# Attention and snake feed-forward on one Trainium2 core: a rebuilt opening (queries loaded first, keys in three parts, bias bands read from SBUF)

## The chip, the cores and the metric

The kernel runs on one core of one Trainium2 chip. The metric is the device time of one execution in microseconds (us); lower is better. A core has five engines with their own instruction streams: TensorE (PE in the profile, its weight loads PEld), VectorE (DVE), ScalarE (ACT), GpSimd (POOL) and SyncE (SP). Loads and stores are DMA transfers; here SP, ACT and POOL issue them, each on its own queue, and the 16 DMA engines of the core carry them out. SBUF is the on-chip memory with 128 partitions, PSUM the eight banks into which TensorE writes.

## The reference

Attention with a relative position bias over 8 batches, 8 heads, 576 positions and 64 dimensions per head, and a feed-forward layer with the snake activation behind it. In short:

```python
scores = q @ k.T / sqrt(64)                        # [8, 8, 576, 576]
scores = scores + bias_table[bucket(|i - j|)]      # 32 buckets, one value per head
attn = softmax(scores)
x = (attn @ v) as [8 * 576, 8 * 64]                # 4608 tokens, 512 wide
h = x @ w_in                                       # 512 -> 2048
g = h + sin(alpha * h)**2 / (alpha + 1e-9)
out = g @ w_out                                    # 2048 -> 512
```

All inputs and the output are float32 in HBM; the kernel computes in float16 with float32 sums. From a distance of 128 on, all positions fall into the last bucket. So exp(score + bias) is computed as exp(score) times a factor exp(bias - bias of the last bucket) that differs from 1 only in a band around the diagonal: the bias costs one multiply of each tile's band.

## The kernel before, in words

**Blocks.** The outer loop `t` runs over the 8 batches. For each: transposed keys and queries (`kTs`, `qTs`, with two heads, a "pair", on the 128 partitions), scores, exponentials, band multiply, product with `v`, normalization, and a transposed result in `xT`; then w_in, sine, square and g for 512 tokens, and w_out. Scores are computed with keys on the partitions. Unit "A" of a pair is one chunk of 128 keys against 512 queries for both heads, its exponential has 1024 columns (L749). Unit "C" takes the last 64 keys of both heads at once, through a block-diagonal copy `kts` of these keys (the key tail). Batch 0 has four pairs with four A units and one C unit each: twenty exponentials.

**Opening of batch 0.** The keys and then the queries of heads 0 and 1 are loaded on SP (`load_nat`, L475) as float32 with six rows on each of 96 partitions, cast to float16 (`cast0` at L510 and the copies at L558, L559), turned by six TensorE transposes (`plan_tr`, L594) and copied out of PSUM (L583). Pairs 1 to 3 come through POOL's queue already cast (`load_pair`, L475) and are turned at L600. Meanwhile ACT turns the bias table into `e_sb`: eight partitions, one per head, with 512 factors as a function of the distance (`plan_table`; the exponential at L639, the copy at L649).

**Bands.** A multiply needs the factor of key p and query x at every place, which depends on x - p alone. So partition p of the band tile `m2r` has to hold the row of `e_sb` shifted by p. Such a skewed view is a matter of addresses: L650 writes `e_sb` to HBM five times over (`e_dram`), and L516 and L523 read it back with a step of 1 per partition: three loads for `m2r`, two for `mhr` (the bands of the key tail). These five are issued on SP, and behind them the float32 values of heads 4 to 7 (`load_v32`, L462), which POOL casts (L465).

**Order.** The order of instructions on each engine is computed when the program is built. `Plan` holds tasks with the engines that may run them, an estimated duration, dependencies, a priority (lower goes first) and an earliest time `nb`. A list scheduler places them on the estimated clock of each engine; each engine then runs its list strictly in that order, and waits where an input is not there. Constants named `T_...` are the earliest times (of loads that the plan does not model), `WARM...` govern padding matmuls on zeros (`zz`) that fill gaps of TensorE in the opening, and `pad` puts such matmuls behind a task. A task's DMA issues go to the queue of their engine in the order in which the tasks are placed. The attention of batch 0 is laid out in `plan_att0`: a fixed list of units (`runs`), then one product with `v` per pair (`plan_av`), whose last steps are the normalization (L1056, L1057), four transposes (L1088) and a copy into `xT` (L581, L583). In the later batches that transposition is done by a DMA from SP (L1079).

**Behind the opening.** The first w_in matmul of batch 0 is placed at `T_W0` or later; POOL issues the weights (`load_w_in16`, L481) at `T_WI`, after a small copy that waits for band 2 of `m2r` (L675), and the keys and queries of batch 1 (`loads2`) at `T_RST`.

Of the kernel before, what the change touches and what calls it, by code (L numbers as in the profile page):

```python
# [224 lines left out]
WARM_END = 22.0  # L225
# [9 lines left out]
T_CL = 24.5  # L235
# [6 lines left out]
T_V0 = (5.8, 6.4, 8.9, 9.6)  # L242
T_P3 = 7.0
T_VA = (10.5, 11.0)
T_VB = 19.5
V_AT = {1: (4, 5, 6, 7)}
V_PRI = -1000
T_AL = (10.0, 560)
# [3 lines left out]
T_TP = ((150, 150), (650, 650), (1500, 1500))  # L252
# [3 lines left out]
T_LD = 33.0  # L256
# [4 lines left out]
PRE = -100  # L261
# [8 lines left out]
T_WS = (43.0, 48.3, 48.3, 48.3)  # L270
# [7 lines left out]
NORM0 = 900  # L278
SQ = {"ACT": 0.51, "DVE": 0.355}
T_V = ((15.5, 19.0), (50.0, 50.0))  # L280
T_TR1 = ((32.0, 33.5), (35.0, 36.5))
T_W = (25.5, 30.5)
T_WO = (40.5, 43.0, 45.7, 48.3)
WARM0 = 8
# [3 lines left out]
WARM_FROM = 7.3  # L288
# [19 lines left out]
def kernel(  # L308
# [11 lines left out]
    nc = tc.nc  # L320
# [14 lines left out]
    NE = 5  # L335
# [8 lines left out]
    e_dram = nc.dram_tensor("e_dram", [NE, 4 * H, EW], F16, kind="Internal")  # L344
# [50 lines left out]
    )  # L395
    nat2x = tp.tile([128, NF * DM], F16, name="nat2", tag="g", bufs=2)
# [30 lines left out]
    def bank(b, n=1):  # L427
        k = b.banks[0]
        return pb[:, k, :] if n == 1 else pb[:, k : k + n, :]
# [43 lines left out]
    def load_nat(dst, h0, h1, src, eng):  # L473

        eng.dma_start(out=dst, in_=src[h0:h1].rearrange("h (p i) d -> p h (i d)", i=SI))  # L475
# [33 lines left out]
    def cast0(kq, eng):  # L509
        eng.tensor_copy(  # L510
            out=natb[:, kq], in_=nat0[:, kq].rearrange("s two (i d) -> s i two d", i=SI)
        )

    def load_m2r(eng, h0, h1, r):

        eng.dma_start(  # L516
            out=m2r[:, h0:h1],
            in_=bass.AP(tensor=e_dram, offset=EW * (4 * H * r + h0), ap=[[1, 128], [EW, h1 - h0], [1, XW]]),
        )

    def load_mhr(eng):
        for z in range(2):
            eng.dma_start(  # L523
                out=mhr[64 * z : 64 * z + 64],
                in_=bass.AP(tensor=e_dram, offset=EW * (4 * H * (1 + z) + z) + 192,
                            ap=[[1, 64], [2 * EW, NP], [1, 192]]),
            )
# [28 lines left out]
    cast0(0, nc.vector)  # L556
    x0 = nat0[:, 1].rearrange("s two (i d) -> s i two d", i=SI)
    nc.vector.tensor_copy(out=natb[:, 1, :, 0], in_=x0[:, :, 0])  # L558
    P_.tensor_copy(out=natb[:, 1, :, 1], in_=x0[:, :, 1])  # L559
# [70 lines left out]

    def plan_table():
# [12 lines left out]

        def mm(e):
            full(bank(b)[0:H, 0:EW], tabE, phi_sb, True, True)

        def cp(e):
            nc.scalar.activation(out=e_sb, in_=bank(b)[0:H, 0:EW], func=AF.Copy)  # L649
            nc.scalar.dma_start(  # L650
                out=e_dram.ap()[:, 0:H].rearrange("r h x -> h r x"),
                in_=e_sb.unsqueeze(1).to_broadcast([H, NE, EW]),
            )
# [8 lines left out]
        plan.add({"ACT": 1.1}, cp, [x], -1100, use=[b])  # L662
# [144 lines left out]
    def plan_att0(g, gates, gate):  # L807
# [3 lines left out]
        runs = ((a, "A", 0), (a, "A", 1), (a, "A", 2), (a, "C", 0), (a, "A", 3),  # L811
                (b, "A", 0), (b, "A", 1), (b, "C", 0), (b, "A", 2), (b, "A", 3))
        exps, head = [], []
        for i, unit in enumerate(runs):
            base = PB + 3200 * g + 300 * i
# [189 lines left out]
    def plan_av(t, parts, u, ub, done, base, dma):  # L1005
# [457 lines left out]
    tr = {(0, 0, kq): plan_tr(0, 0, kq, -1000, T_FIRST[kq]) for kq in range(2)}  # L1463
# [97 lines left out]
```

## Time and profile before

| | us |
|---|---|
| median of three runs | 364.12 |
| lowest and highest | 364.03, 364.92 |
| profiled execution, first to last instruction (span) | 361.6 |
| median less span | 2.5 |
| TensorE busy, all of the span | 356.0 |
| ACT busy, all of the span | 316.3 |
| DVE busy, all of the span | 306.1 |
| POOL busy, all of the span | 93.2 |

The profiled execution's own time is not listed apart from the span; what lies around the span is taken as the 2.5 us of the table. In the profile a row of the time line reads: start, duration, engine, line, operation, output <- inputs, shapes, count, and in brackets the idle time of the engine just before and what ended it. SPq, POOLq and ACTq are the DMA issues on these engines. A group such as "x14" joins neighbouring instructions of one kind; its duration runs from the first start to the last end. A row of the DMA issues ends with the median time from issue to landing. TensorE's busy time counts matmuls in flight, so that a full engine may still wait briefly. The granted clock of TensorE was 1.00 throughout.

### The profile page before, as it was taken

The page shows a single profiled execution, that of the slowest core. Times are in us where ns is not written, and L with a number is a line of the kernel's source. Part 1 is how long each engine was busy: PE and PEld are TensorE (multiplying, and loading weights), DVE is VectorE, ACT ScalarE, POOL GpSimd, SP SyncE. Part 2 cuts the span into 40 slices and gives each one's busy share as a digit, 9 for nine tenths or more (in the row PEclk, how much of TensorE's full clock was granted, in tenths as well). Part 3 has the DMA queues.
Part 4 walks back from the last instruction along what each step waited for, and adds up shares of the span by engine and source line. Part 5 has one row for each costly group of instructions (what it writes and reads, how often), then busy time and mean ns, then how long its engine had stood idle before and what let it go on. Part 6 is the DMA issues. An engine that isn't in the chain of part 4 may idle for free.

```text
span 361.6 us, 9613 instructions
## 1 busy us (share of the span) xinstructions
PE 356.0 (98%) x3811; PEld 218.4 (60%) x3811; DVE 306.1 (85%) x749; ACT 316.3 (87%) x436; POOL 93.2 (26%) x135
## 2 busy tenths in 40 slices
PE   8999999999999999999999999999999999999996
PEld 4564445644575447884684458545787467456685
DVE  4887888989977998699978997899869986999982
ACT  2998999999998999899989999899989998996811
POOL 8577450064000820055001900091006000000000
PEclk9999999999999999999999999999999999999999
DMA  9999999789724994299918992699339322001023
GB/s 167 206 200 188 207 160 134 142 83 124 120 48 104 138 150 101 55 158 143 137 34 159 110 169 55 127 136 143 87 81 158 66 57 54 15 3 59 31 76 101
DMA packets 150157, 40.53 MB, mean 112 GB/s; under 512 B 137224, under 2 KB 145504, under 8 KB 150112
## 3 DMA queue, kind: packets, MB, share of 16 engines
q0 software_dynamic: 96064, 17.67, 60.7%
q1 hardware_dynamic: 53872, 22.16, 26.1%
q8 instruction: 30, 0.49, 0.6%
q10 hardware_dynamic: 176, 0.09, 0.1%
q14 instruction: 15, 0.12, 0.1%
HBM read 37.73 MB, written 16.56 MB: 150 GB/s over the span
## 4 chain that ended last, share of the span: by engine, by line
PE 94%; DMA 2%; ACT 1%; DVE 1%; SPq 0%; issue 0%; DVEq 0%
PE pb L500 93%; DMA mhr<-e_dram 1%; ACT u L749 1%; DMA e_dram<-e_sb 1%; PE pb L600 1%; PE pb L1088 1%; DVE u L780 1%; DVE s L1057 0%; SPq L523 0%; ACT e_sb L649 0%; PE pb L594 0%; ACT xT L581 0%; SPq L516 0%; DVE outs L1314 0%; DVE zz L551 0%
## 5 line engine op out<-in xcount | busy, mean ns | idle before, releaser
L749 ACT ACTIVATE u<-pb 128x1024 f16<-128x1024 f32 (+1 forms) x146 | 136.8, 1020 | 6.2 <-PE pb L500 4.9
L500 PE MATMUL pb<-xT,w_in 128*128 128x512 f16 (+4 forms) x704 | 128.6, 340 | 0.3 <-ACT xT L581 0.3
L1146 DVE SCALAR_TENSOR_TENSOR g<-sq,inv_a,pb 128x512 f16<-128x512 f16 x144 | 101.4, 744 | 3.8 <-ACT sq L1139 1.8
L1132 ACT ACTIVATE s<-pb,alphaT 128x512 f16<-128x512 f32 x144 | 92.9, 693 | 12.4 <-PE pb L500 11.6
L500 PEld LDWEIGHTS <-w_in 128*128 128x128 f16 x704 | 64.5, 98 | 56.0 <-issue 0.8
L500 PE MATMUL pb<-w_out,g 128*128 128x512 f16 (+1 forms) x416 | 83.5, 339 | 0.0
L500 PEld LDWEIGHTS <-g 128*128 128x128 f16 x552 | 50.8, 98 | 34.8 <-issue 5.2
L780 DVE TENSOR_TENSOR u<-u,m2r 128x512 f16<-128x512 f16 (+1 forms) x128 | 61.5, 488 | 9.9 <-ACT u L749 9.2
L500 PEld LDWEIGHTS <-u 128*128 128x128 f16 x1280 | 55.9, 97 | 9.6 <-issue 4.9
L1139 ACT ACTIVATE sq<-s 128x512 f16<-128x512 f16 x76 | 47.5, 640 | 2.0 <-DVE g L1146 1.1
L445 POOL COPY kt<-kT 64x256 f16<-64x256 f16 x12 | 5.2, 430 | 168.0 <-DMA kT<-staged_k 167.7
L500 PE MATMUL pb<-v,u 128*128 128x65 f16 x1024 | 43.8, 193 | 0.0
L500 PE MATMUL pb<-qT,kT 64*128 64x64 f16 (+1 forms) x512 | 42.1, 285 | 0.8 <-DVE qT L583 0.3
L1141 DVE TENSOR_TENSOR sq<-s 128x512 f16<-128x512 f16 x68 | 28.4, 427 | 11.3 <-ACT s L1132 10.4
L500 PEld LDWEIGHTS <-kT 64*128 64x128 f16 x512 | 17.2, 94 | 20.5 <-issue 13.1
L500 PE MATMUL pb<-vh,u 128*128 128x130 f16 x128 | 28.3, 221 | 0.2 <-DVE s L1057 0.2
L1000 DVE TENSOR_TENSOR xn<-pb,rd 128x384 f16<-128x384 f32 (+2 forms) x53 | 26.0, 490 | 1.8
L450 POOL DMA_DIRECT2D v<-in_v_dram x28 | 24.7, 895 | 3.1 <-DMA nat<-in_k_dram 1.8
L1459 ACT ACT_TABLE_LOAD x15 | 19.2, 1283 | 0.3
L749 ACT ACTIVATE nat<-pb 128x1024 f16<-128x1024 f32 (+1 forms) x24 | 18.8, 820 | 0.0
L999 DVE RECIPROCAL rd<-pb 128x6 f32<-128x6 f32 (+2 forms) x53 | 9.9, 187 | 8.2 <-PE pb L500 7.0
L500 PE MATMUL pb<-wsum,g 128*128 128x256 f16 (+1 forms) x136 | 16.7, 267 | 0.0
(100 smaller groups left out, 311.7 us busy)
## 6 DMA issues: line engine op xcount, KB each, us to landing
out_dram<-outs SPq DMA_DIRECT2D x28, 256.0 KB, 3.0
v<-in_v_dram POOLq DMA_DIRECT2D x28, 128.0 KB, 4.8
staged_k<-in_k_dram POOLq DMA_DIRECT2D x6, 576.0 KB, 8.6
staged_q<-in_q_dram POOLq DMA_DIRECT2D x6, 576.0 KB, 12.1
w_in<-in_moe_w_in_dram POOLq DMA_DIRECT2D x4, 512.0 KB, 9.1
w_out<-in_moe_w_out_dram POOLq DMA_DIRECT2D x4, 512.0 KB, 13.5
out_dram<-outs SPq DMA_DIRECT2D x16, 128.0 KB, 1.7
w_out<-in_v_dram SPq DMA_DIRECT2D x6, 128.0 KB, 5.1
```

The source lines that it names most:

```text
L445: nc.gpsimd.tensor_copy(out=kts[t % 2][r, :, r], in_=kTs[t % 2][r, :, 512:S])
L450: nc.gpsimd.dma_start(out=vs[t % 2][:, c, :, 0:D], in_=vp[128 * c : 128 * c + 128],)
L500: nc.tensor.matmul(out=out, lhsT=lhsT, rhs=rhs, start=start, stop=stop, skip_group_check=go_on)
L749: nc.scalar.activation(out=o, in_=x, func=AF.Exp, scale=0.125)
L780: nc.vector.tensor_tensor(out=io, in0=io, in1=m2[:, 2 * p : 2 * p + 2, x0 : x0 + hi - lo], op=ALU.mult)
L999: nc.vector.reciprocal(out=r, in_=x[:, :, :, D])
L1000: nc.vector.tensor_tensor(out=xn[:, 0:n].rearrange("p c (z d) -> p c z d", z=2), in0=x[:, :, :, 0:D], in1=r.unsqueeze(3).to_broadcast([128 ...
L1132: nc.scalar.activation(out=s16.v, in_=h.v, func=AF.Sin, scale=alphaT[:, f : f + 1])
L1139: nc.scalar.activation(out=sq.v, in_=s16.v, func=AF.Square)
L1141: k_of(e).tensor_tensor(out=sq.v, in0=s16.v, in1=s16.v, op=ALU.mult)
L1146: nc.vector.scalar_tensor_tensor(out=gcell[b].v[:, f, :], in0=sq.v, scalar=inv_a[:, f : f + 1], in1=h.v, op0=ALU.mult, op1=ALU.add,)
L1459: nc.scalar.preload_act_table_set(name)
```

## The change

Only the opening is touched, and constants of the order.

- The queries of heads 0 and 1 are loaded first, then the keys in three parts: rows 0 to 143 and 144 to 287 with two rows on each of 72 partitions, and the remaining 288 with four rows. alpha's load moves from ACT's queue to SP's, behind them; the constants' load on ACT goes ahead of the table's.
- `plan_first` replaces `cast0` and `plan_tr` for pair 0. The query cast is split over DVE and ACT, and so is the copy of the turned queries. Key parts 0 and 1 are cast on DVE, part 2 on POOL; part 0 is copied by ACT, the others by DVE. The key tail's copies move from POOL to DVE. The first exponential needs the queries and key part 0, the second part 1 as well, and only from the third on the whole of the keys.
- `e_dram` and its write are gone. Each head's band is read directly out of its row of `e_sb` by a DMA with the skewed address pattern: eight for `m2r`, eight for `mhr`, all on SP, ahead of the values of heads 4 to 7.
- The order of units in a pair is A, A, C, A, A for all pairs of batch 0.
- For pairs 0 and 1 of batch 0 (`DT0 = 2`) the four TensorE transposes and the copy into `xT` are replaced by one DMA transpose on SP.
- Five instead of eight padding matmuls of 512 columns at the start; earliest times and priorities are set anew, most behind the opening by 2.0 us earlier.

```diff
-WARM_END = 22.0
+WARM_END = 20.0
-T_START = 4.0
+T_START = 3.4
-T_W0 = 24.5
+T_W0 = 22.5
-T_WI = 16.8
-T_TAB = 5.2
+T_WI = 13.4
+T_TAB = 4.0
-T_FIRST = (4.75, 5.95)
-T_PAIR = ((7.9, 8.5), (9.3, 10.2), (11.6, 12.3))
+E_ON = {"ACT": 0.52}
+T_Q0 = 3.95
+T_KP = (4.3, 4.6, 5.2)
+K_CAST = ({"DVE": 0.26}, {"DVE": 0.26}, {"POOL": 0.9})
+K_COPY = ("ACT", "DVE", "DVE")
+K_PRI = (-1880, -1870, 10)
+DT0 = 2
+RUN0 = 'aacaa aacaa'
+U0 = 200
+T_PAIR = ((6.6, 7.2), (8.8, 9.4), (11.0, 11.6))
-T_M2 = (14.6, 15.4, 16.6, 17.2)
-T_MH = 15.4
-T_RST = 25.0
+T_M2 = (9.0, 11.0, 12.5, 12.5)
+T_MH = 10.0
+T_RST = 23.0
-T_VB = 19.5
+T_VB = 17.5
-NORM0 = 900
+NORM0 = 1700
-WARM0 = 8
+WARM0 = 5
-WARM_FROM = 7.3
+WARM_FROM = 6.0
...
-    e_dram = nc.dram_tensor("e_dram", [NE, 4 * H, EW], F16, kind="Internal")
...
+    def skew(h, off, rows, w):
+
+        x = e_sb[h : h + 1]
+        return bass.AP(tensor=x.tensor, offset=x.offset + off, ap=[[EW, 1], [1, rows], [1, w]])
+
+    def load_m2r(eng, h):
+        eng.dma_start(out=m2r[:, h], in_=skew(h, 0, 128, XW))
+
+    def load_mhr(eng, h):
+        z = h % 2
+        eng.dma_start(out=mhr[64 * z : 64 * z + 64, h // 2], in_=skew(h, 192, 64, 192))
...
-    load_nat(nat0[:, 0], 0, 2, k[0], nc.sync)
     load_nat(nat0[:, 1], 0, 2, q[0], nc.sync)
+    for (k0, n_), x in zip(KP, kf):
+        nc.sync.dma_start(
+            out=x, in_=k[0, 0:2, k0 : k0 + SR * n_].rearrange("h (p i) d -> p h (i d)", i=n_)
+        )
+    nc.scalar.dma_start(out=phi_x, in_=phi_h.ap())
     nc.scalar.dma_start(out=tabN, in_=bias_table)
-    nc.scalar.dma_start(out=phi_x, in_=phi_h.ap())
-    nc.scalar.dma_start(out=alphaN, in_=moe_alpha.rearrange("(f p) -> f p", p=128))
+    nc.sync.dma_start(out=alphaN, in_=moe_alpha.rearrange("(f p) -> f p", p=128))
     load_v32(0)
     load_v32(1)
...
+    def plan_first():
...
+        x = nat0[:, 1].rearrange("s two (i d) -> s i two d", i=SI)
+        qs = [cast(natb[:, 1, r], x[:, r], {e: d}, T_Q0, -1990)
+              for r, e, d in ((slice(0, 3), "DVE", 0.36), (slice(3, 6), "ACT", 0.38))]
+        m, q0 = turn([natb[:, 1, i] for i in range(SI)], SN, qTs[0][:, 0, :], qs, -1890,
+                     [("DVE", 0, 3), ("ACT", 3, 6)])
+        m.pad = ((192,) * PAD_FIRST,)
+        ks = []
+        for i, ((a, n), ec, ex) in enumerate(zip(KP, K_CAST, K_COPY)):
+            x = kf[i].rearrange("s two (i d) -> s i two d", i=n)
+            y = cast(kb[i], x, ec, T_KP[i], -1980 + i)
+            m, z = turn([kb[i][:, j] for j in range(n)], SR, kTs[0][:, 0, a : a + SR * n], [y], K_PRI[i],
+                        [(ex, 0, n)])
+            m.pad = ((192,) * PAD_FIRST,)
+            ks.append(z[0])
...
+        tl = plan.add({"DVE": 0.3}, tail, kr, T_TL)
+        tr[(0, 0, 0)] = ks, [tl]
+        tr[(0, 0, 1)] = q0, q0
+        tr["first"] = [ks[:1] + q0, ks[:2] + q0]
...
-            nc.scalar.activation(out=e_sb, in_=bank(b)[0:H, 0:EW], func=AF.Copy)
-            nc.scalar.dma_start(
-                out=e_dram.ap()[:, 0:H].rearrange("r h x -> h r x"),
-                in_=e_sb.unsqueeze(1).to_broadcast([H, NE, EW]),
-            )
-            load_m2r(nc.sync, 0, 2, 0)
-            load_mhr(nc.sync)
-            load_m2r(nc.sync, 2, 4, 3)
-            load_m2r(nc.sync, 4, H, 4)
+            copy_on(e, e_sb, bank(b)[0:H, 0:EW])
+            for p in range(NP):
+                load_m2r(nc.sync, 2 * p)
+                load_m2r(nc.sync, 2 * p + 1)
+                load_mhr(nc.sync, 2 * p)
+                load_mhr(nc.sync, 2 * p + 1)
             for h in range(4, H):
                 load_v32(h)
...
+            if g == 0 and i < 2:
+                deps = gates + tr["first"][i]
...
-        if dma:
+        if dma or wide and p0 < DT0:
 
             def turn(e):
+                if wide:
+                    nc.sync.dma_start_transpose(
+                        out=xT[:, p0, x0 : x0 + 512].rearrange("d (c q) -> d c q", c=4),
+                        in_=xn.v.rearrange("p c d -> p (c d)"))
+                    return
```

`turn` of `plan_first` is the six (or two, or four) transposes of one part with its copies; the units' priorities in `plan_att0` now step by `U0`.

More of the change, by code (lines that the diff above doesn't have):

```diff
@@ L629, in plan_tr, with cast, turn, mm @@
         return [x], [plan.add({"POOL": 0.4 if t == 0 else 0.5}, tail, [x], pri + 30)]
+    def plan_first():
+        def cast(o, i, engs, nb, pri):
+            return plan.add(engs, lambda e: copy_on(e, o, i), [], pri, nb=nb)
+        def turn(parts, rows, dst, deps, pri, copies):
+            b, c = Buf("mo"), Cell()
+            n = len(parts)
+            def mm(e):
+                c.v = bank(b).bitcast(F16)
+                for i, x in enumerate(parts):
+                    nc.tensor.transpose(
+                        out=c.v[:, rows * i : rows * i + rows], in_=x, identity=id_sb[0:rows, 0:rows]
+                    )
+            m = plan.add({"PE": 0.02 + n * T_TURN * rows / 96}, mm, deps, pri, new=[b])
+            made = []
+            for e, a, z in copies:
+                def cp(e, a=a, z=z):
+                    copy_on(e, dst.rearrange("d (p i) -> d p i", i=n)[:, :, a:z],
+                            c.v[:, 0 : n * rows].rearrange("d (i p) -> d p i", i=n)[:, :, a:z])
+                w = (z - a) * rows
+                made.append(plan.add({"DVE": 0.07 + w / 830.0} if e == "DVE" else {"ACT": 0.07 + w / 1150.0},
+                                     cp, [m], pri, use=[b]))
+            return m, made
+        x = nat0[:, 1].rearrange("s two (i d) -> s i two d", i=SI)
[12 more added lines that the diff above has]
+            ks.append(z[0])
+        kr = ks[2:]
+        def tail(e):
+            for z in range(2):
+                r = slice(64 * z, 64 * z + 64)
+                k_of(e).tensor_copy(out=kts[0][r, 0, r], in_=kTs[0][r, 0, 512:S])
+        tl = plan.add({"DVE": 0.3}, tail, kr, T_TL)
+        tr[(0, 0, 0)] = ks, [tl]
+        tr[(0, 0, 1)] = q0, q0
+        tr["first"] = [ks[:1] + q0, ks[:2] + q0]
@@ L1462 @@
     PB = 0
[L1463 removed]
+    tr = {}
+    plan_first()
     vdone, lds, spans = [], [], {}
```

69 lines of the change are left out of this document (30 added, 39 removed).

## The prediction

> **What bounds the kernel now.** I read the page first (busy shares and the chain that ended last), then busy time by stretches, then the opening instruction by instruction.
>
> ```profile
> span 361.6 us, 9613 instructions
> PE 356.0 (98%) x3811; PEld 218.4 (60%) x3811; DVE 306.1 (85%) x749; ACT 316.3 (87%) x436; POOL 93.2 (26%) x135
> ...
> PE 94%; DMA 2%; ACT 1%; DVE 1%; SPq 0%; issue 0%; DVEq 0%
> ```
>
> Busy us by stretches; the columns are PE, PEld, DVE, ACT, POOL, then granted clock, DMA share and GB/s:
>
> ```profile
> 8.45:14.43 5.98, 5.95 (x96) 3.27 (x95) 4.85 (x9) 5.81 (x7) 4.18 (x11) 1.00 1.27 172
> 14.43:19.60 5.17, 4.75 (x58) 2.74 (x58) 4.58 (x13) 5.17 (x7) 3.22 (x6) 1.00 1.03 226
> 33.00:50.00 17.00, 17.00 (x194) 8.25 (x191) 14.97 (x32) 16.74 (x28) 10.80 (x16) 1.00 1.51 193
> 46.00:357.00 311.00, 310.90 (x3300) 193.33 (x3300) 269.79 (x671) 277.97 (x380) 61.59 (x66) 1.00 0.85 100
> ```
>
> The chain lies 94% on PE. PE fills the last 311 us (310.90 of it), so nothing the change touches shortens that part; it can only start it sooner or later. Before it ACT is the full engine: 5.81 of 5.98, 5.17 of 5.17, then 16.74 of 17.00. So the opening is a run of exponentials on ACT, and its worth is when the first one starts, whether the run stays closed, and what follows the last.
>
> ```profile
> 0.81 0.40 SPq L475 DMA_DIRECT2D natx<-in_k_dram  x1
> 1.27 0.43 SPq L475 DMA_DIRECT2D natx<-in_q_dram  x1
> ...
> 3.92 0.64 DVE L510 CAST natx<-natx 96x768 f16<-96x768 f32 x1 [1.15 <-DMA natx<-in_k_dram]
> 4.97 0.69 PE L594 MATMUL pb<-id_sb,natx 96*128 96x96 f16 x6
> 5.32 0.35 DVE L558 CAST natx<-natx 96x384 f16<-96x384 f32 x1 [0.76 <-DMA natx<-in_q_dram]
> 5.35 0.69 POOL L559 CAST natx<-natx 96x384 f16<-96x384 f32 x1 [0.74 <-DMA natx<-in_q_dram]
> 6.74 0.43 PE L594 MATMUL pb<-id_sb,natx 96*128 96x96 f16 x6
> 7.21 0.76 DVE L583 COPY qT<-pb 128x576 f16<-128x576 f16 x1 [0.75 <-PE pb L594]
> 8.02 0.39 PE L500 MATMUL pb<-qT,kT 64*128 64x512 f16 x2 [0.27 <-DVE qT L583]
> 8.45 1.02 ACT L749 ACTIVATE u<-pb 128x1024 f16<-128x1024 f32 x1 [1.01 <-PE pb L500]
> 9.64 11.66 ACT L749 ACTIVATE u<-pb 128x1024 f16<-128x1024 f32 x14 [0.17 <-PE pb L500]
> 21.57 4.26 ACT L749 ACTIVATE u<-pb 128x1024 f16<-128x1024 f32 x5 [0.27 <-PE pb L500]
> 25.66 0.69 DVE L1057 TENSOR_TENSOR s<-pb,rd 128x512 f16<-128x512 f32 x1
> 26.27 0.42 DVE L780 TENSOR_TENSOR u<-u,m2r 128x512 f16<-128x512 f16 x1
> 28.97 5.99 PE L500 MATMUL pb<-xT,w_in 128*128 128x512 f16 x27 [0.26 <-ACT xT L581]
> ```
>
> The queries come second and set the first exponential: cast from 5.32, turned at 6.74, copied at 7.21 to 7.97, multiplied at 8.02, exponential at 8.45. Twenty exponentials end at 21.57 + 4.26 = 25.83, 17.38 us later. From there to the closed run of w_in matmuls (28.97) it is 3.14 us of one chain. The bias bands, the table and the transfers are carried by further views. Who waited for whom on SP, and the DMA issues with their time to landing:
>
> ```profile
> SPq L516 <- DMA e_dram<-e_sb: 7.7, 1, 7.7
> ...
> natx<-in_k_dram SPq DMA_DIRECT2D x1, 288.0 KB, 3.1
> natx<-in_q_dram SPq DMA_DIRECT2D x1, 288.0 KB, 4.0
> tabN<-in_bias_table_dram ACTq DMA_DIRECT2D x1, 1.0 KB, 2.5
> phi_sb<-phi_const ACTq DMA_DIRECT2D x1, 36.0 KB, 3.8
> w_out<-in_v_dram SPq DMA_DIRECT2D x6, 128.0 KB, 5.1
> xT<-xn SPq DMA_TRANSPOSE x47, 2.8
> ```
>
> The instructions in order of time, with the write of the bands' source from the chain as the second line:
>
> ```profile
> 6.85 0.59 ACT L649 ACTIVATE e_sb<-pb 8x512 f16<-8x512 f32 x1 [0.62 <-PE pb L500]
> 7.46 2.94 DMA e_dram<-e_sb
> 10.49 0.37 SPq L516 DMA_DIRECT2D m2r<-e_dram  x1
> 10.90 1.33 SPq L523 DMA_DIRECT2D mhr<-e_dram  x2
> 13.44 3.44 SPq L462 DMA_DIRECT2D w_out<-in_v_dram  x4
> 14.43 1.35 DVE L780 TENSOR_TENSOR u<-u,m2r 128x512 f16<-128x512 f16 x3
> 20.77 0.42 DVE L583 COPY xT<-pb 128x512 f16<-128x512 f16 x1
> 21.09 1.68 POOL L465 CAST v<-w_out 128x256 f16<-128x256 f32 x4
> 24.82 1.02 PE L500 MATMUL pb<-xT,w_in 128*128 128x512 f16 x4
> 26.39 0.74 POOL L475 DMA_DIRECT2D nat<-in_k_dram  x1
> ```
>
> **The change part by part.**
>
> *Queries first.* The first load on SP lands at 0.81 + 3.1 = 3.91 (the cast row agrees: 3.92), the second at 1.27 + 4.0 = 5.27. Queries in first place gain 1.36 us. Half of their cast goes to DVE (0.35, the same size as L558) and half to ACT, which has no such row of its own there; 0.4 by the 8x512 copy's 0.59 as upper end. So 4.35 to 4.5 instead of 6.04 (5.35 + 0.69 on POOL). Six transposes take 0.43 to 0.69: 4.95 to 5.2. The copy, 0.76 for 576 columns, is halved over DVE and ACT, near 0.42: with 0.1 us of hand-over at each step the queries stand near 5.6.
>
> *Keys in three parts.* Rows 0 to 143 and 144 to 287 are 72 KB each and follow the queries at once; 288 KB took 1.36 us between the two landings, so a quarter takes 0.35: about 4.3 and 4.7, the rest 5.3 to 5.7. First part: cast on DVE near 0.25 behind its query half, two transposes, 144 columns copied on ACT behind its query half: 5.9. The first score matmul then stands near 6.0 instead of 8.02, and the first exponential, 0.43 later, near 6.45 instead of 8.45: 2.0 us. The ends: 6.1 if nothing queues, 7.1 if PE stands behind the table. phi now goes out first on ACT's queue and lands at 0.81 + 3.8 = 4.6; the matmul that needs it ranks ahead of all else on PE, so the query transposes may wait until about 5.
>
> *What moves with them.* Two more loads on SP, and alpha's from ACT's queue, push the first two value heads back by 3 x 0.43 = 1.3 us. Their readers are POOL's casts and the first attention product, which waits for bands in any case; no cost. POOL, which issues loads, also gets the third part's cast, 0.9 us (0.69 x 512/384), near 5.6 to 6.6; the loads queued behind it are for pair 3, not wanted before 19. The key tail, now on DVE, must be done for the third exponential (order A, A, C, A, A): 6.6, then four transposes, 288 columns copied, tail 0.3, matmul 0.39, gives about 8.3, where ACT comes free near 8.3. I count 0.1, ends 0 and 0.4.
>
> *Warm-up.* Three 512-column matmuls fewer ahead of the transposes.
>
> ```profile
> 1.26 3.92 PE L500 MATMUL pb<-zz 128*128 128x512 f16 x10 [1.26 <-DVE zz L551]
> ```
>
> These ran near 0.42 us each while two 512-column score matmuls later took 0.39 together, with a granted clock of 1.00 in every stretch. If PE stays at the slow pace to the first score, transposes cost 0.69 instead of 0.43 and two score matmuls 0.85 instead of 0.39: 0.7 us late at most. I take 0, since the loss is only on the first scores and the padding matmuls continue. The Trainium skill (TensorE: Matmul & The Clock Gate, Part 1) asks for about 3.4 us of sustained work before full speed; five matmuls are 2.1 us of it, so by the page the slow case is the likelier, and the sum would be 0.7 us worse.
>
> *Bands from SBUF.* Gone are the write (2.94) and SP's wait for it (7.7). Instead e_sb, copied on ACT in the same 0.59 and now near 6.4, is read directly by sixteen issues. By 0.37 (one with 256 runs) to 0.67 (half of 1.33) each, they hold SP until 12.4 to 17.2, against 13.4 now. The bands need not be early: DVE began them at 14.43 and the last one (26.27) still came right after the last exponential. Behind them on SP stand four value heads (3.44 to issue, then 5.1), read by POOL at 21.09, in the new schedule at 19.1. At the short end the first lands at 12.4 + 5.1 = 17.5, the fourth at about 20.4, as it is cast; at the long end 22.3, which would hold back the products of pairs 2 and 3 by 3 us. A single head has half the runs of the 0.37 row; I take the short end, 0.
>
> *Two pairs turned by DMA.* PE loses eight 128-column transposes, DVE two copies of 0.42. In their place stand 2.8 us of landing. Pair 1 would be there near 23.1, beside a first reader at 24.82 - 2 = 22.8. PE has other work then; 0, ends 0 and 1. SP has nothing else to do at that time except the value heads just named.
>
> *End of the opening.* The last multiply (26.27) sat behind pair 2's normalization (0.69 from 25.66, released by ACT at about 25.9). Normalizations now rank later; 0 to 0.4 gained, I count 0.1. Weights and the next batch are issued earlier (w_in by 3.4 us, the next queries and keys by 2), and their POOL order is otherwise kept: the 26.39 load moves with POOL's free time, 24.4. If it did not move, the transposes that read it would give the gain back.
>
> **Sum.** -2.0 (first exponential) + 0.1 (third) - 0.1 (end) = -2.0, then 0.1 for new small waits: -1.9. Everything behind the opening keeps its length, so the span is 359.7. The profiled execution's time beside its span is not shown apart; the runs' median stands 2.5 above the span, and I keep that: 362.2.
>
> **The rivals.**
>
> *The gain is given back.* The run of exponentials starts early but is opened by a load behind it: value heads late on SP (up to 3 us), the third key part, a cold PE (0.7), or the next batch's keys. For it: DMA share is above 1 in both opening stretches shown. Against it: in the stretch 14.43 to 19.60 ACT never waits although the bands come at 14.43. On 362.2 these put 0.7 to 3 us: about 363.0 to 365.2.
>
> *Bands drip out of a few lines.* Every band is now read from one row of e_sb by all DMA engines at once. The one read of e_sb in the trace is the write of 40 KB in 2.94, 0.44 above the 1 KB load's 2.5: some 90 KB/us from eight rows. All bands are 8 x (96 + 24) = 960 KB; at that rate they take 10.6 us and land between 11.7 and 19.6 (from 6.5 + 2.5), still ahead of pair 3's exponentials. DVE needs about 2.2 us for a pair, so they must be there by 21.8, which is 75 KB/us: below that this rival decides. At half the measured rate, 45 KB/us, the last band lands at 30.3, 8.5 late: 362.2 + 8.5 = 370.7, slower than before. Against it: no row shows a read slowed this way. The Trainium skill (SBUF — State Buffer, Door 1: The DMA port swizzle) has four neighbouring partitions share one port of about 27 GB/s, here heads 0 to 3 on one and 4 to 7 on another; by that, in one queue, 36 us and an end near 386. The 40 KB row is short of settling it, since two such ports would also have passed it in 0.75.
>
> *More than forecast.* The bands' early arrival empties DVE and the tail of 3.14 us shrinks by 0.4 or more: below 361.3.
>
> **How the numbers follow.** Gain carried through 0.64 (361.3 to 363.0), given back 0.16, bands drip 0.17, more 0.03. Three runs differ by 0.9 us, so 0.3% (1.1 us, 363.0 to 365.2) is what counts as a change: faster 0.67, same 0.16, slower 0.17. The range 361.2 to 365.2 leaves out the slow bands and the far gain.
>
> **What would show it.** First exponential at 6.1 to 7.1, the twentieth ending near 23.9, closed w_in matmuls from about 27.0, PE full from there on. Wrong if DVE's first band multiply stands after 12 or the bands' landing grows from head to head (drip); if the value casts on POOL start after 20 (SP queue); if the exponentials show new gaps (third key part, cold PE); or if 27.0 is reached and the stretch behind it, closed now (17.00 of 17.00), shows PE waiting for weights or for the next batch's keys.

## The result and the profile after

| | before | after |
|---|---|---|
| median, us (four runs each) | 364.14 | 394.00 |
| lowest and highest | 364.03, 364.92 | 393.59, 394.61 |
| profiled execution, span | 361.6 | 392.8 |

The ratio is 1.0812, with a 95% interval from 1.0778 to 1.0847: the changed kernel is 8% slower. The forecast was 362.2, and its range ended at 365.2.

The busy shares and the chain that ended last, of the kernel after:

```profile
PE 365.3 (93%) x3799; PEld 223.2 (57%) x3799; DVE 305.2 (78%) x751; ACT 318.6 (81%) x439; POOL 92.2 (23%) x133
...
PE 86%; SPq 8%; DMA 4%; ACT 1%; issue 0%; POOL 0%; ACTq 0%; DVE 0%
```

SP's queue, which rounded to 0% of the chain before, now carries 8% of it. Busy time of the part behind the opening (columns as in the prediction):

```profile
80.00:389.00 309.00, 308.90 (x3268) 192.66 (x3266) 268.05 (x664) 275.16 (x377) 56.97 (x65) 1.00 0.81 99
```

PE fills this part as it did before (308.90 of 309.00, against 310.90 of 311.00). The whole loss lies in the opening. Its instructions in order of time:

```profile
4.15 0.52 ACT L588 ACTIVATE natx<-natx 96x384 f16<-96x384 f32 x1 [1.15 <-DMA natx<-in_q_dram]
4.72 0.24 PE L516 MATMUL pb<-tabN,phi_sb 32*32 32x8 f32 x2 [0.82 <-DMA tabN<-in_bias_table_dram]
5.24 0.69 PE L650 MATMUL pb<-id_sb,natx 96*128 96x96 f16 x6
7.13 0.30 PE L650 MATMUL pb<-id_sb,natx 72*128 72x72 f16 x2
7.24 0.52 PE L516 MATMUL pb<-zz 128*128 128x192 f16 x2
7.69 0.61 PE L516 MATMUL pb<-qT,kT 64*128 64x512 f16 x2
8.07 0.60 POOL L590 CAST natx<-natx 72x512 f16<-72x512 f32 x1 [3.72 <-DMA natx<-in_k_dram]
8.34 1.02 ACT L808 ACTIVATE u<-pb 128x1024 f16<-128x1024 f32 x1 [0.51 <-PE pb L516]
9.10 5.59 SPq L535 DMA_DIRECT2D mhr<-e_sb  x2
10.67 1.02 ACT L808 ACTIVATE u<-pb 128x1024 f16<-128x1024 f32 x1 [1.31 <-PE pb L516]
18.06 0.90 DVE L839 TENSOR_TENSOR u<-u,m2r 128x512 f16<-128x512 f16 x2 [5.68 <-DMA m2r<-e_sb]
29.26 0.42 DVE L839 TENSOR_TENSOR u<-u,m2r 128x512 f16<-128x512 f16 x1 [4.07 <-DMA m2r<-e_sb]
33.74 4.68 SPq L535 DMA_DIRECT2D mhr<-e_sb  x2
38.46 10.23 SPq L478 DMA_DIRECT2D w_out<-in_v_dram  x4
39.10 0.90 DVE L839 TENSOR_TENSOR u<-u,m2r 128x512 f16<-128x512 f16 x2 [6.11 <-DMA m2r<-e_sb]
48.41 0.43 DVE L839 TENSOR_TENSOR u<-u,m2r 128x512 f16<-128x512 f16 x1 [6.76 <-DMA m2r<-e_sb]
60.36 1.84 ACT L1200 ACTIVATE s<-pb,alphaT 128x512 f16<-128x512 f32 x3 [0.48 <-PE pb L516]
```

Line numbers have moved: L531 and L535 issue the bands of `m2r` and `mhr`, L839 is the band multiply, L808 the exponential, L478 the value heads' load, L481 their cast, L588 and L590 copies and casts on ACT and on other engines, L650 the turns of the first pair, L516 any other matmul, L1200 the sine. Read the four L839 rows that wait for `m2r`: they stand some 10 us apart (18.06, 29.26, 39.10, 48.41), one for each pair of heads. SP is held all that time: the issues of the sixteen bands run until 33.74 + 4.68 = 38.42, the four value heads stand behind them, and the first sine, at 29.38 before, starts at 60.36, 31 us later. The list of waits up to 62 us says the same (engine, reader <- what it waited for: total us, times, longest):

```profile
DVE u L839 <- DMA m2r<-e_sb: 22.6, 4, 6.8
...
POOL v L481 <- DMA w_out<-in_v_dram: 10.5, 1, 10.5
PE pb L607 <- DVE alphaT L750: 7.0, 1, 7.0
...
DVE qT L590 <- ACT qT L588: 0.5, 1, 0.5
```

DVE runs its list in order, so what stands behind a band multiply waits with it. The `alphaT` line shows this: a PE matmul is held 7.0 us by a small DVE copy that the bands do not concern. In this way late bands also stop the exponentials on ACT.

And the DMA issues of the kernel after, with the median time from issue to landing at the end:

```profile
m2r<-e_sb SPq DMA_DIRECT2D x8, 96.0 KB, 10.7
mhr<-e_sb SPq DMA_DIRECT2D x8, 24.0 KB, 13.3
```

A pair's bands are 240 KB, and three pairs follow each other from 18.06 to 48.41: 10.1 us each, about 24 KB/us. The prediction's rival of dripping bands decides below 75 KB/us.

One more thing differs from before. The granted clock of TensorE, 1.00 in every stretch of the kernel before, falls here (the third number from the end):

```profile
46.00:60.00 14.00, 7.33 (x90) 5.67 (x90) 4.61 (x12) 2.83 (x5) 7.16 (x18) 0.63 0.60 102
```

It reads 0.50 from 41 to 44 and again from 49 to 57; PE had waited 2.6 us before its work at 40.89 and 5.3 before that at 49.73. So the work behind such a wait also runs slower. Up to 40 the clock reads 1.00, though two scores take 0.61 there (7.69), not the 0.39 of before; this comes back below.

But the bands are one part of a change of many parts. What each is worth, and whether the drip is really a matter of where `e_sb` lies, was tried on the chip.

### The profile page after: what moved, and what is told of

It reads as the page before. It is cut to its first block, busy times and chain, and to the rows that moved or that the text cites. A ratio compares the mean times of both kernels' runs of the same rounds, so it can differ in the third digit from the quotient of the medians.

```text
span 392.8 us, 9616 instructions
## 1 busy us (share of the span) xinstructions
PE 365.3 (93%) x3799; PEld 223.2 (57%) x3799; DVE 305.2 (78%) x751; ACT 318.6 (81%) x439; POOL 92.2 (23%) x133
## 4 chain that ended last, share of the span: by engine, by line
PE 86%; SPq 8%; DMA 4%; ACT 1%; issue 0%; POOL 0%; ACTq 0%; DVE 0%
PE pb L516 84%; SPq L535 5%; DMA w_out<-in_v_dram 4%; SPq L531 2%; DMA tabN<-in_bias_table_dram 1%; PE pb L607 1%; PE pb L1156 0%; ACT u L808 0%; POOL v L481 0%; PE pb L650 0%; ACT e_sb L588 0%; ACTq L548 0%; DVE outs L1382 0%; PE pb L1044 0%
## 5 line engine op out<-in xcount | busy, mean ns | idle before, releaser
L808 ACT ACTIVATE u<-pb 128x1024 f16<-128x1024 f32 (+1 forms) x146 | 137.7, 1015 | 25.2 <-PE pb L516 23.9
L516 PE MATMUL pb<-xT,w_in 128*128 128x512 f16 (+4 forms) x704 | 128.7, 341 | 0.0
L1200 ACT ACTIVATE s<-pb,alphaT 128x512 f16<-128x512 f32 x144 | 92.8, 692 | 12.4 <-PE pb L516 11.6
L516 PEld LDWEIGHTS <-w_in 128*128 128x128 f16 x704 | 64.6, 98 | 55.4
L839 DVE TENSOR_TENSOR u<-u,m2r 128x512 f16<-128x512 f16 (+1 forms) x128 | 61.4, 486 | 31.4 <-DMA m2r<-e_sb 22.6
L516 PE MATMUL pb<-w_out,g 128*128 128x512 f16 (+1 forms) x416 | 83.5, 339 | 0.0
L516 PEld LDWEIGHTS <-u 128*128 128x128 f16 x1280 | 59.5, 101 | 20.9 <-issue 16.5
L516 PEld LDWEIGHTS <-g 128*128 128x128 f16 x552 | 50.8, 98 | 34.8 <-issue 5.2
L516 PE MATMUL pb<-v,u 128*128 128x65 f16 x1024 | 47.2, 199 | 2.9 <-POOL v L481 2.9
L516 PE MATMUL pb<-qT,kT 64*128 64x64 f16 (+1 forms) x512 | 44.8, 297 | 0.0
L516 PE MATMUL pb<-vh,u 128*128 128x130 f16 x128 | 29.4, 230 | 7.9 <-DVE s L1120 7.9
L516 PEld LDWEIGHTS <-kT 64*128 64x128 f16 x512 | 16.9, 95 | 21.2 <-issue 14.2
L1527 ACT ACT_TABLE_LOAD x15 | 19.2, 1283 | 0.3
L808 ACT ACTIVATE nat<-pb 128x1024 f16<-128x1024 f32 (+1 forms) x24 | 18.8, 822 | 0.0
L607 PE MATMUL pb<-id_sb,nat 96*64 96x96 f16 x168 | 7.1, 239 | 11.1 <-DVE alphaT L750 7.0
```

Of the source, the lines that this page charges most:

```text
L516: nc.tensor.matmul(out=out, lhsT=lhsT, rhs=rhs, start=start, stop=stop, skip_group_check=go_on)
L607: nc.tensor.transpose(out=c.v[64 * z : 64 * z + 64, x : x + SN], in_=(nat1 if t == 0 else nat2)[:, kq, h, D * i : D * i + D], identity=id_ ...
L808: nc.scalar.activation(out=o, in_=x, func=AF.Exp, scale=0.125)
L839: nc.vector.tensor_tensor(out=io, in0=io, in1=m2[:, 2 * p : 2 * p + 2, x0 : x0 + hi - lo], op=ALU.mult)
L1200: nc.scalar.activation(out=s16.v, in_=h.v, func=AF.Sin, scale=alphaT[:, f : f + 1])
L1527: nc.scalar.preload_act_table_set(name)
```

## The experiments

Two ladders were run: from the kernel after downwards, one part taken back at a time, and single parts put into the kernel before. The edits are shown abridged; constants of several lines may stand on one.

**Bands by HBM again.** The kernel after with `e_dram`, its write and the five reads of before, and their earliest times.

```diff
-T_WI = 13.4, T_M2 = (9.0, 11.0, 12.5, 12.5), T_MH = 10.0
+T_WI = 16.0, T_M2 = (14.6, 15.4, 16.6, 17.2), T_MH = 15.4
+    e_dram = nc.dram_tensor("e_dram", [NE, 4 * H, EW], F16, kind="Internal")
```

> The changed kernel with one part undone: the bands go through HBM again (five copies written, five loads), with the earliest times that belong to it. Theory (the bands drip because every read of a band goes to one place in SBUF): the drip is gone, DVE's first band multiply stands near 14.5 to 15.5 and the time falls by 28 to 31 us, to 363 to 366. Rival (the other parts cost too: third key part late, cold TensorE, value heads late): the time stays 3 us or more above 366.

Measured: 379.54 (ratio to before 1.0408, 1.0341 to 1.0475). The drip goes, and with it 14.5 us; the other 15 us stay. So the rival held, and by far more than the 3 us it named. DVE's first band multiply stands at 19.94 and not at 14.5 to 15.5. From its time line:

```profile
12.20 0.61 PE L518 MATMUL pb<-qT,kT 64*128 64x512 f16 x2
...
22.06 2.92 POOL L499 DMA_DIRECT2D w_in<-in_moe_w_in_dram  x4
...
27.21 3.93 SPq L1149 DMA_TRANSPOSE xT<-s  x2
...
37.53 1.44 PE L518 MATMUL pb<-xT,w_in 128*128 128x512 f16 x3 [8.41 <-DMA xT<-s]
```

Busy time of one stretch of it (columns as before):

```profile
12.00:16.00 4.00, 4.00 (x26) 1.41 (x24) 1.17 (x5) 3.56 (x4) 1.68 (x4) 1.00 1.07 169
```

Two new suspects: PE waits 8.41 us for a pair turned by DMA, and two score matmuls take 0.61 instead of 0.39 at 12.20, though PE is full in that stretch (4.00 of 4.00) and the granted clock reads 1.00 there.

**Where the bands are read from.** Three kernels that differ in the source partitions alone. `e_sb` is computed alike on all 128 partitions, and a band is read from 128 of them, from eight neighbours, or from eight that lie four apart: bytes, queue and order stay. The skew is left out, so the bands are not the reference's. The last three lines are the three variants:

```diff
-        x = e_sb[h : h + 1]
-        ap=[[EW, 1], [1, rows], [1, w]]          # the change: the one row of head h
+        in_=e_sb[:, 0:XW]                        # row p from partition p
+        ap=[[EW, 8], [1, rows // 8], [1, w]]     # from partitions 0 to 7
+        ap=[[4 * EW, 8], [1, rows // 8], [1, w]] # from partitions 0, 4, ... 28
```

> The changed kernel, with the table copied to all 128 partitions (same instructions, wider operands) and each of the sixteen band loads reading row p from partition p. It leaves the skew out: the bands are not the reference's. Number, size and run length of the transfers are as in the changed kernel. Theory (one place in SBUF is the limit): each band lands in 3 to 5 us, the time is 362 to 367. Rival (sixteen small SBUF to SBUF loads with 768-byte runs on SP's queue are slow by themselves): it stays at 388 or more.

> As the run from 128 rows, but every band is read from the eight neighbouring partitions 0 to 7, sixteen rows from each; skew left out, the bands are not the reference's. Theory (a group of four neighbouring partitions shares one port): two groups, twice the rate of one row, about 50 GB/s in place of 25; all bands take some 20 us instead of 40, the time is 372 to 380. Rival (the single partition is the limit): eight times the rate, the time is as with eight partitions four apart, 362 to 368.

> As the run from eight neighbours, but the eight partitions are 0, 4, 8 to 28: same number of partitions, same runs, same DMA engines, skew left out, the bands are not the reference's. Theory (groups of four): eight groups, so four times the rate of the eight neighbours; the time is 362 to 368. Rival (the single partition is the limit, or the number of DMA engines is): no different from the eight neighbours, within 2 us.

Measured, one run each: 374.96, 381.04 and 374.19; one row for each head, the kernel after, has 394.00. The absolute times lie higher than expected; the runs below take other parts apart that cost too. The differences answer the question: eight rows four partitions apart are as good as 128, eight neighbours cost 6.9 us more, with the same bytes and runs. SP's issues from the time line of the first (128 rows), beside the two that take 5.59 from 9.10 on in the kernel after:

```profile
17.93 1.24 SPq L531 DMA_DIRECT2D mhr<-e_sb  x2
19.22 8.05 SPq L478 DMA_DIRECT2D w_out<-in_v_dram  x4
```

The same of the second (eight neighbours), and DVE's multiplies that wait for its bands:

```profile
9.57 3.77 SPq L535 DMA_DIRECT2D mhr<-e_sb  x2
15.09 0.90 DVE L841 TENSOR_TENSOR u<-u,m2r 128x512 f16<-128x512 f16 x2 [2.76 <-DMA m2r<-e_sb]
20.76 0.42 DVE L841 TENSOR_TENSOR u<-u,m2r 128x512 f16<-128x512 f16 x1 [1.18 <-DMA m2r<-e_sb]
26.29 0.90 DVE L841 TENSOR_TENSOR u<-u,m2r 128x512 f16<-128x512 f16 x2 [1.60 <-DMA m2r<-e_sb]
```

The first three pairs stand 5.6 us apart here, so 240 KB come at about 43 KB/us, not quite twice the 24 from one row. If each partition alone were the limit, eight would give far more than that. So a read out of few neighbouring partitions is slow. The Trainium skill (SBUF — State Buffer, Door 1: The DMA port swizzle) says that four neighbouring partitions share one port of about 27 GB/s; the 24 KB/us (GB/s) from one row, the 43 from two groups of four and the gap between the second and the third kernel agree with it. Even with the port out of the way, the band issues take 0.62 us each (1.24 for two) and start the value heads at 19.2 (128 rows) and 18.7 (eight, four apart) instead of 13.44. That is later than the "long end" of 17.2, where the prediction had taken the short one.

**Bands from SBUF alone**, in the kernel before, the mirror of the first run: `load_m2r` and `load_mhr` as in the diff of the change, the constants as before.

```diff
-            load_m2r(nc.sync, 0, 2, 0); load_mhr(nc.sync); load_m2r(nc.sync, 2, 4, 3); load_m2r(nc.sync, 4, H, 4)
+            for p in range(NP):
+                load_m2r(nc.sync, 2 * p); load_m2r(nc.sync, 2 * p + 1)
+                load_mhr(nc.sync, 2 * p); load_mhr(nc.sync, 2 * p + 1)
```

> The kernel before with one part of the change alone: the bands read from their rows of the table in SBUF by sixteen loads. Theory (a row of SBUF is read at 25 GB/s: 960 KB in 39 us, and four value heads behind it): the time is 386 to 394, and the landings of the bands lie some 9 us apart per pair. Rival (the slow bands of the changed kernel come from what else it loads at that time): 364 to 372.

Measured: 396.38 in one run, 32 us above before and 2 us beyond what the theory named. The part alone costs as much as the whole change. A load of another queue comes late beside it: PE waits for the keys of pair 3, which POOL loads and for which PE did not wait in the kernel before. Its list of waits:

```profile
DVE u L772 <- DMA m2r<-e_sb: 17.6, 3, 8.4
PE pb L498 <- POOL v L463: 13.4, 1, 13.4
...
PE pb L595 <- DMA nat<-in_k_dram: 7.8, 1, 7.8
```

**Bands by HBM, without DMA turns.** The first run above, and all pairs turned by TensorE again.

```diff
-DT0 = 2
+DT0 = 0
```

> The run with bands by HBM (379.5 us), and also the turns of pairs 0 and 1 back on TensorE. In that run TensorE waited 8.4 us for a DMA turn that stood behind the w_in load. Theory (the DMA turns cost what their landing shows): the wait goes and the time falls by 5 to 8 us, to 371 to 375; it is less than 8.4 because the products of pairs 2 and 3 and the w_in landing come next. Rival (w_in itself is what is late, the DMA turn only ended last): within 2 us of 379.5.

Measured: 373.63 (1.0251, 1.021 to 1.0291), 5.9 us less.

**DMA turns alone**, in the kernel before.

```diff
-        if dma:
+        if dma or wide and p0 < DT0:                        # DT0 = 2, as in the change
```

> The kernel before with one part of the change alone: the turns of pairs 0 and 1 by DMA. Theory (a DMA turn issued while w_in is being loaded lands only behind it): the two turns land 6 us or more after their issue, the first w_in matmul waits for them, the time rises by 2 to 6 us, to 366 to 370. Rival (the wait of 8.4 us came from w_in being issued 5 us later there): 363.5 to 364.7, no change.

Measured: 376.65 (1.032, 1.0247 to 1.0392), 12 us above before and more than expected. From its time line:

```profile
18.30 2.93 POOL L482 DMA_DIRECT2D w_in<-in_moe_w_in_dram  x4
...
20.67 5.53 SPq L1079 DMA_TRANSPOSE xT<-s  x2
```

In its view of `xT` in the opening, the time from issue to landing:

```profile
DMA to landing us min/median/max: 10.9/11.0/11.2
```

PE waits 8.5 us for these two. 11 us, where the later batches' turns took 2.8 in the rows of the prediction. Around them POOL issues the 2 MB of w_in (18.30 to 21.23). Is it that load, or the turn itself?

**DMA turns ahead of the weights.** The same kernel with w_in issued behind the turns.

```diff
-T_WI = 16.8, T_W0 = 24.5
+T_WI = 24.0, T_W0 = 29.0
```

> The kernel before with the first two pairs turned by DMA, as in the run of that part alone, but the w_in load issued at 24.0 (placed) instead of 16.8, so behind both turns, and the first w_in matmul placed at 29.0 instead of 24.5. Theory (a DMA turn that is issued behind the 2 MB load of w_in waits for that load's packets on the shared DMA engines): the two turns land within 5 us of their issue instead of 11.0, PE waits less than 1 us for xT from a turn instead of 8.5, and it waits for w_in instead, so that the span is no shorter than the 375.0 of that run by more than 4 us. Rival (a DMA turn in the opening is slow for a reason of its own: the bands, the value heads, its first use): the turns still land 9 us or more after their issue, and PE waits for xT.

Measured: 371.88 in one run (before 364.55 beside it). From its time line:

```profile
20.62 3.73 SPq L1079 DMA_TRANSPOSE xT<-s  x2
...
25.35 2.91 POOL L482 DMA_DIRECT2D w_in<-in_moe_w_in_dram  x4
...
33.27 10.14 PE L501 MATMUL pb<-xT,w_in 128*128 128x512 f16 x34 [1.86 <-DMA w_in<-in_moe_w_in_dram]
```

The landing of the two turns:

```profile
DMA to landing us min/median/max: 2.5/3.3/4.2
```

The turns land in 3.3 us and nobody waits for them: so it was the load of w_in, not the turn itself, that made them slow. PE now waits for the weights (issued 7 us later), and the loss is 7 us instead of 12. The span, 369.9, is 5.1 us shorter than in the run before, a little more than the 4 that the theory allowed. Either order of turns and weights costs.

**Warm-up.** The run by HBM and without DMA turns, and eight starting matmuls instead of five.

```diff
-WARM0 = 5
+WARM0 = 8
```

> As the previous run, and eight padding matmuls of 512 columns at the start in place of five. Theory (with five, TensorE stays at the slow pace: two score matmuls 0.61 us and not 0.39, to 24 us): the score matmuls take 0.39 again from the first on, the run of exponentials shortens by 4 to 5 us, the time falls to 366 to 371. Rival (the pace comes from something else in the new order, such as the half-height score matmuls): no change, within 1 us of the previous run.

Measured: 369.66 (1.0147, 1.0122 to 1.0173), another 4.0 us. The group of the 32 score matmuls in the opening (busy us, mean ns), with five:

```profile
L518 PE MATMUL pb<-qT,kT 64*128 64x512 f16 x32 | 8.5, 549 | 0.0
```

The same group with eight:

```profile
L518 PE MATMUL pb<-qT,kT 64*128 64x512 f16 x32 | 6.3, 414 | 0.8 <-ACT u L816 0.8
```

And from the time line with eight, the exponentials:

```profile
7.81 12.80 ACT L816 ACTIVATE u<-pb 128x1024 f16<-128x1024 f32 x15 [0.59 <-PE pb L518]
```

**Five starting matmuls alone**, in the kernel before.

```diff
-WARM0 = 8
+WARM0 = 5
```

> The kernel before with one edit: five padding matmuls at the start in place of eight. Theory (fewer leave TensorE slow through the opening): the score matmuls show about 0.6 us for two, the time rises by 3 to 5 us, to 367 to 369. Rival (the other paddings make up for it): 364, within 1 us.

Measured: eight executions that fall into two groups, 364.33 to 364.63 (four) and 368.57 to 370.15 (four). The profiled one belongs to the second. From its time line, the matmuls on zeros at the start and the first two scores:

```profile
1.27 2.63 PE L500 MATMUL pb<-zz 128*128 128x512 f16 x7 [1.27 <-DVE zz L551]
...
8.46 0.61 PE L500 MATMUL pb<-qT,kT 64*128 64x512 f16 x2
```

With five, the same kernel takes as long as before or 4 to 5.5 us longer. In the profiled execution two scores take 0.61 up to 24.62 and 0.39 from 25.70 on. No profile of the first group was taken; that TensorE reaches its full pace in time there is inferred from the times. The granted clock reads 1.00 all along, so the slow PE is seen only in the duration of one kind of matmul. (In the run with bands from SBUF alone two scores also take 0.61, at 20.51, where the clock reads 0.50.) The Trainium skill (TensorE: Matmul & The Clock Gate, Part 1) asks for about 3.4 us of sustained work before full speed. The group at the start lasts 2.63 us here and 3.92 in the kernel before, one on each side of that figure; the trace agrees. What lets four of eight executions with five come out fast is open.

**Ranks of the turns.** The last kernel of the ladder with the priorities of pairs 1 to 3 as before.

```diff
-T_TP = ((150, 750), (1150, 1350), (2200, 2400))
+T_TP = ((150, 150), (650, 650), (1500, 1500))
```

> The run with bands by HBM, no DMA turn and eight warm-ups (369.7 us), and the priorities of the turns of pairs 1 to 3 as in the kernel before. In that run ACT stood 3.9 us between the fifteenth and sixteenth exponential: TensorE waited 2.7 us for DVE's copy of pair 3's queries, which the order puts behind eight band multiplies. Theory (the new ranks only suit bands that come early): that wait goes, the time falls by 2 to 4 us, to 366 to 368. Rival (the bands by HBM are late whatever the rank): within 1 us of 369.7.

Measured: 366.14 (1.0045, 1.0014 to 1.0076). With the ranks of the change PE waits for a later pair's queries, and the exponentials, closed until 20.6, show a hole of 3.91 us. The time line of the kernel with eight starting matmuls, ahead of this edit:

```profile
21.64 0.22 PE L518 MATMUL pb<-vh,u 128*128 128x130 f16 x1 [2.69 <-DVE qT L595]
...
24.52 2.43 ACT L816 ACTIVATE u<-pb 128x1024 f16<-128x1024 f32 x3 [3.91 <-PE pb L518]
```

And with the ranks of before:

```profile
21.04 1.94 ACT L816 ACTIVATE u<-pb 128x1024 f16<-128x1024 f32 x2 [1.51 <-PE pb L518]
```

The largest hole is 1.51, and the first sine comes 2.5 us earlier (32.49, not 34.99). The granted clock, 0.50 from 22 to 25 with the ranks of the change, stays at 1.00. The remaining 1.8 us (1.0045) are not taken apart.

**The first pair alone**: queries first, keys in three parts, casts on two engines; everything else as before, but for the earlier start of the plan and of the padding (`T_START`, `WARM_FROM`) and the duration planned for the table's copy (`E_ON`). Then the same with the third key part cast on DVE and the queries copied by DVE in one piece.

```diff
-K_CAST = ({"DVE": 0.26}, {"DVE": 0.26}, {"POOL": 0.9});  [("DVE", 0, 3), ("ACT", 3, 6)]
+K_CAST = ({"DVE": 0.26}, {"DVE": 0.26}, {"DVE": 0.5});   [("DVE", 0, 6)]
```

> One part of the change alone: queries first, keys in three parts, casts and copies on two engines; all else as in the kernel before (bands by HBM, eight warm-ups, order, ranks and times of the later work, turns on TensorE). Theory (this part is worth what the first exponential gains, and the run of exponentials behind it stays closed): the first exponential at 7.6 to 8.0 and not 8.45, the time 363.3 to 363.8, that is 0.3 to 0.8 us less. Rival (the third key part and the key tail open the run by as much): 364.0 to 365.0.

> As the previous run, but the third key part is cast on DVE in place of POOL, and the queries are copied by DVE in one piece (in the changed kernel DVE's half began only when ACT's half was done). Theory (POOL's cast is late because of POOL's issues, and the split copy gains nothing): the key tail comes 0.5 us earlier, the time is the previous run's or up to 0.4 us less. Rival (DVE becomes full): 0.3 us or more above the previous run.

Measured: 372.39 (1.0204, 1.0158 to 1.025) and 367.04 (1.0069, 1.0039 to 1.0099). They start their exponentials at 8.83 and 8.74. The busy time behind the opening, of the first:

```profile
62.00:360.00 298.00, 292.06 (x3074) 180.78 (x3071) 258.59 (x633) 257.39 (x353) 56.91 (x64) 1.00 0.76 95
```

In the second PE is full there (298.00 of 298.00). What stands ahead of the first exponential in the first of the two:

```profile
8.27 0.52 ACTq L717 DMA_DIRECT2D e_dram<-e_sb  x1
8.83 1.02 ACT L816 ACTIVATE u<-pb 128x1024 f16<-128x1024 f32 x1 [0.59 <-PE pb L655]
```

Neither brings the first exponential below the 8.45 of before. Its scores are there in time (at 7.55, for 0.39), but ACT first copies the table (7.65 to 8.24) and issues the write of the bands, until 8.79. The plan expects 0.52 us for both, the value that belongs to the copy without a write; the kernel before plans 1.1. In the second kernel the write's issue ends at 8.70 and the exponential follows at 8.74. So the theory of an earlier first exponential was not put to a fair test, and 8 and 2.7 us are not the price of this part alone.

The first of the two also loses 6 us behind the opening, in holes of PE of up to 0.5 us that the second doesn't have. The edit lies in the first pair alone, but the order of PE's instructions differs between the two over most of the program: the planner's clocks were shifted, and everything later was placed anew. Which of its decisions makes the holes is not settled.

No kernel tried was faster than the one before.

## Why the prediction was wrong

**The ladder.** From 394.0: bands by HBM -14.5, turns by TensorE -5.9, eight starting matmuls -4.0, ranks as before -3.5, remainder 1.8 to 364.3. Single parts in the kernel before: bands +32, turns +12, five starting matmuls 0 or +4 to 5.5, first pair +8 or, with another assignment, +2.7 (with the table's write in its way). These don't add up to 30; that a late band covers part of the other losses is likely, but no run shows it apart.

*The granted clock: no term in the sum.* The prediction had it at 1.00 in every stretch of the kernel before. PE's busy time times the missing share of the clock, added up over the first 80 us, is an estimate of what its fall costs: 4.1 us of the 30 in the kernel after, 7.6 with bands from SBUF alone, 2.8 with DMA turns alone. It is 2.1 with bands by HBM and 0 without the DMA turns, 1.7 with eight starting matmuls and 0 with the ranks as before. By this estimate some 2 us each of the steps of 5.9 and 3.5 are the clock behind a wait, not the wait. Between eight neighbours and eight apart it makes no difference (1.8 and 2.0).

*Bands from SBUF: wrong, and the largest miss.* The failed step is "I take the short end, 0", and under it the estimate of "some 90 KB/us from eight rows". That row was a write of 40 KB in which a fixed time dominates; it was taken as evidence of the rate at which one row can be read. The sum itself holds no term for the time of the reads. The rate was 24 KB/us, the mechanism that of the rival, with 0.17. The rival's own price for a half rate, 370.7, was also too low; the end near 386 that it gave by the port's figure lies closer to the 394.0 measured. SP's hold was predicted too short in the same step: not 0.37 to 0.67 an issue, but 2.8 (half of 5.59) at 9.10, while the transfers ahead of it were slow.

*Two pairs turned by DMA: wrong.* "2.8 us of landing" came from later batches, where nothing like 2 MB of weights stands ahead. In the opening it was 11.0, and 3.3 with the weights moved behind. The step had looked at SP's queue alone, not at what POOL's has in flight at that time.

*Warm-up: wrong.* "I take 0" had as its upper end 0.7, counting only the first scores. The slow pace lasts through most of the opening; the term is 0 or 4 to 5.5 us. That "the padding matmuls continue" doesn't end it: at 12.20, with PE full, the scores still take 0.61.

*Queries first: mostly wrong.* The queries landed nearly as predicted (their cast begins at 4.15, forecast 3.91). The first exponential came at 8.34 instead of 6.45, the gain 0.1 instead of 2.0. The step that failed is the sum "then stands near 6.0 instead of 8.02" with its end "7.1 if PE stands behind the table". PE does stand behind it: the table's product is released by its load at 4.72, and the turns follow at 5.24, forecast 4.95, at 0.69. Then DVE's half of the queries waits 0.5 us for ACT's and is done at 6.97. The first score still has to wait: ahead of it PE takes the turn of the second key part (7.13) and that turn's two padding matmuls (7.24, 0.52), which the sum had left out. It stands at 7.69 and takes 0.61. With a PE at full pace the exponential is at 7.81 in the ladder, directly behind the issue of the bands' write on ACT: 0.6 us gained.

*The third key part on POOL: wrong in time.* It begins at 8.07, not 5.6, after a wait of 3.72 for its load. The step that failed is the landing, "the rest 5.3 to 5.7", taken from 1.36 us for 288 KB: the second part's cast begins at 5.74 (landing forecast at 4.7), the third's load is there only at 8.07. The run of exponentials is open from its second member on (1.31 us ahead of the one at 10.67), before the first band is wanted.

*What held.* In the kernel after, PE is as full behind 80 us as before (308.90 of 309.00), so that part kept its length. As a rule this failed: in the first pair alone PE lost 6 us there. The weights and the next keys did not come earlier: they were issued at 26.17 and 56.48, not at 13.7 and 24.4, behind the late bands and value heads. Also right was the reading that PE, full behind the opening, hands on what the opening loses (31 us at the first sine, 31.2 in the span), and the signs named for a drip (bands landing from head to head, a first multiply after 12) were the ones seen.

## What to carry to other kernels

A skewed or replicated read of SBUF must be costed by its source partitions: spread the source over partitions that lie four apart, or go through HBM, before asking DMA to fan one row out to 128. When a part is tried alone, its planned durations have to fit it too, or the trial measures the plan. Before moving work from a full engine to DMA, look at which transfers are in flight at that time, on any queue. And where an unknown price decides the sign, a row of another kind (here a write) is no estimate of it: a single kernel with that edit alone would have shown +32 us.

## What was not expected of the hardware

- Bands of 96 KB, each read from one partition's row, take 10.7 us (median) to land, 4.3 from 128 rows; together they come at 24 KB/us. Eight rows four partitions apart do as well as 128 (374.19 and 374.96 us), eight neighbours reach 43 KB/us and 381.04 us. With bands from SBUF alone PE also waited 7.8 us for keys that POOL's queue was loading.
- While such transfers drip, the issuing engine is held as well: 5.59 us for two issues, against 1.24 with 128 source rows.
- A DMA transpose of a [128, 512] tile lands in 3.3 us, or in 11.0 behind a 2 MB load on another queue.
- 2.6 us of starting matmuls leave the time open (364.3 to 364.6, or 368.6 to 370.2), at a granted clock of 1.00 in both; in the one profiled, of the slower group, two scores take 0.61 and not 0.39 up to 24.62.
- Behind waits of PE the granted clock read 0.50 for some us of work: in the run with DMA turns alone five w_in matmuls took 2.29 us there (0.46 each), against 27 in 5.99 (0.22 each) in the kernel before.
